# A long-convolution and MLP kernel: k's transposing loads moved to SP's queue, products of zeros at the start, V's write as one transfer, and a new written-out order

## The chip, the cores and the metric

The kernel runs on one core of a Trainium2 chip. The metric is the time of one execution in device microseconds (us); of several executions the median is taken. A profiled execution gives, besides its time, its span from the first to the last instruction, and a trace.

## The reference

Two layers are applied twice, with the same weights and the same k and v (S = 2048 tokens, D = 512, F = 1376, everything bf16):

```python
def _A_ref(q, k, v, shift_k, ssm_k, ssm_D):
    for t in range(ks):                       # ks = 4
        k_shift = k_shift + k_pad[:, t:t + S, :] * shift_k[:, ks - 1 - t][None, None, :]
    kv = k_shift * v
    # y = causal convolution of kv with the filter ssm_k along S, by rfft of length 2S
    y = y + kv * ssm_D[None, None, :]
    return q * y
def _B_ref(x, w1, b1, w2, b2):
    y = _layernorm(x, axis=-1)
    h = _gelu(jnp.einsum("bsd,df->bsf", y, w1) + b1)
    return jnp.einsum("bsf,fd->bsd", h, w2) + b2

x = A_q
x = x + _A_ref(_layernorm(x), ...)
x = x + _B_ref(_layernorm(x), ...)
x = x + _A_ref(_layernorm(x), ...)
x = x + _B_ref(_layernorm(x), ...)
```

The convolution does not depend on x, so its result is computed once and used in both layers.

## The kernel before, in words

Tokens are handled in two halves of 1024 (h = 0, 1). The convolution is a transform in two matrix stages with fixed tables (F, W, M, M2, G), a product with the filter's transform, and the way back; the MLP is two matrix products with gelu between.

Work is cut into some 600 pieces. `plan.add` (L142) notes a piece with its engine and code, and a table of words at the top of the file, ORDER, says in which order the pieces are written (L148). A word is name.engine: P is TensorE, D VectorE, A ScalarE, G GpSimd, S the queue of SyncE (SP), from which the DMA transfers go; digits behind it choose a buffer. Each engine, and each queue, carries out its pieces in the order of the table and waits at a piece until what it needs is there. Names end in e where a piece empties PSUM (L269 to L273).

The pieces that matter here, first at the start:

- **lK00, lK01** load the first half of the filter ssm_k, **lF**, **lG**, **lW**, **lM2**, **lM** the tables, **lv0** the first half of v (1 MB), all through L327. **lk00, lk01** load the first half of k with a transposing DMA (L395 to L398); they are issued from ScalarE's queue. Behind them on ScalarE stands **tab** (L400), a first gelu, which loads the activation table. **lK10, lK11** (L437) bring the filter's second half with transposing transfers, and **KR10, KR11** ("the turns", L442) move it on within SBUF.
- **KT00, KT01** (L427) transpose the filter on TensorE. **K00S0 to K03S1** (L356) are the first stage of its transform, **K0T0 to K0T3** (L370) transposes behind it; VectorE and ScalarE empty PSUM after each (L273 and L271). **dt0, dt1** add ssm_D. **col, cole** turn the short filter shift_k into columns, **dg0 to dg3** (GpSimd, L470) make diagonal matrices of them, and **kv00 to kv03** (L487) make k_shift with these on TensorE; VectorE multiplies with v (L493).
- **KW** (L502) is the second stage for the filter, **wa** ("the swaps", L512) exchange partitions within SBUF, **U** and **X** are the two stages for kv, **T** the products with the filter's transform (L561).

Then, for the second half of the tokens, the way back:

- **V10 to V17** (L583) go from the product to 512 columns; ScalarE empties each (V10e to V17e) into one half of a buffer of 512 KB. **vw10 to vw13** (L592 to L595) write these buffers, two V's each, to a DRAM tensor vd: vw10 that of V10 and V11, up to vw13 that of V16 and V17. **vr10 to vr13** (L603) read vd in another arrangement and need all four writes; **Y10 to Y13** (L614) multiply what they brought.
- The rows go through layers i = 0 to 7, each a group of 512 tokens in one layer. **sa, pa, na, aa, ga, sb, pb, nb, ab** with i and 0 or 2 are the norms and the product with Y. **dw** (L685) writes the normed rows to DRAM tensors lnd, **dr** (L688) reads them back with a transposing DMA, **m1** (L700) and **m2** (L717) are the two matrix products, **ge** (L707) the gelu, **re** (L721) the sum, **st** (L730) the store. A trailing digit counts parts.

For V's write the layout matters: the buffer has 128 partitions, of which the first 64 (par = 0) and the last 64 (par = 1) belong to two interleaved halves of vd:

```python
vdr = [dram.tile([64, 2, NK, D], BF16, name=f"vd{i}") for i in range(2)]
```

So 64 partitions write 64 rows of vd that lie 2 * NK * D elements apart.

Of the kernel before, what the change touches and what calls it, by code (L numbers as in the profile page):

```python
# [9 lines left out]
BF16 = mybir.dt.bfloat16  # L10
# [6 lines left out]
lK01.S lK00.S lF.S lk01.A lG.S lv0.S lK10.S lk00.A KT01.P0 lW.S tab.A lK11.S KT00.P1 KT01e.D dt1.D lM2.S K02S0.P0  # L17
KT00e.D col.P2 K02S0e.A0 K03S0.P3 cole.D K03S1.P1 K03S0e.A1 dt0.D dg0.G K03S1e.D K00S0.P2 K00S1.P0 K00S0e.A2 K01S0.P3
K00S1e.D K01S1.P1 K01S0e.A3 K0T3.P2 dg3.G K01S1e.D K02S1.P0 K0T3e.A K0T0.P3 K02S1e.D KR10.S K0T1.P1 K0T0e.D dg1.G
K0T2.P2 K0T1e.A kv00.P3 K0T2e.D kv03.P0 dg2.G kvm00.D KW01.P2 KW03.P1 KW01e.A kvm03.D kv01.P3 KW03e.A KW02.P2 kvm01.D  # L20
kv02.P0 KW02e.A KW00.P1 kvm02.D U01S0.P3 KW00e.A KR11.S KW04.P2 KW04e.D U01S0e.A0 U00S0.P0 U00S1.P1 U00S0e.A3 U01S1.P3
U00S1e.D wa00.S U02S0.P2 U01S1e.A U03S0.P0 U02S0e.D2 U02S1.P1 U03S0e.A1 U03S1.P3 U02S1e.D KW07.P2 U03S1e.A KW05.P0
ones0.G kS.G KW07e.D KW05e.A KW06.P1 U0T0.P3 KW06e.A U0T2.P2 U0T0e.D4 wa01.S U0T1.P1 U0T2e.D5 X00.P3 X01.P0 U0T1e.D6
X00e.A U0T3.P2 X01e.A lx0.S T00.D0 X04.P3 X02.P1 X02e.A X03.P0 lk11.S T01.D1 X03e.A V00.P1 U0T3e.D6 X04e.A V01.P0 w3.S
T02.D0 V00e.A X06.P3 X07.P2 X06e.A w4.S T03.D1 V02.P1 lk10.S V01e.A T06.D2 X05.P3 X07e.A V03.P0 T04.D0 lM.S X05e.A
V06.P2 T07.D1 V02e.A V04.P3 V03e.A T05.D2 V07.P1 V04e.A sa12.D V05.P0 V07e.A K1S6.P3 lv1.S sa02.D V05e.A w2.S K1S2.P1
# [10 lines left out]
re03.D pb20.G sa22.D m110.P3 ge12.A Tb16.D2 pa22.G m114.P1 ge10.A U1r2.S1 Ta16.D1 lx1.S X10e.A0 X11.P3 nb20.D aa22.D
V16.P0 U1r1.S5 X11e.A1 Tb10.D0 m113.P2 ge14.A ga22.D V16e.A6 m111.P1 Ta10.D1 ge13.A Ta11.D2 V10.P0 ge11.A X17.P2
Tb11.D0 m115.P3 X17e.A0 X14.P1 Ta17.D1 ge15.A V11.P2 V10e.A0 Tb17.D0 m210.P3 X14e.A1 sb22.D V11e.A ab20.A V17.P2
Tb14.D2 pb22.G X15.P1 m212.P0 X15e.A0 dw20.S re10.D vw10.S nb22.D Ta14.D0 V17e.A ab22.A Ta15.D1 V14.P2 X12.P1 Tb15.D0  # L40
dw22.S V14e.A1 vw13.S X12e.A1 Ta12.D2 V15.P2 X13.P1 Tb12.D0 V15e.A dr2.S X13e.A0 Ta13.D1 V12.P2 vw12.S Tb13.D0 V12e.A5
sa30.D V13.P2 m213.P1 V13e.A sa42.D vw11.S re12.D pa42.G m211.P2 pa30.G na42.D sa40.D aa42.A m121.P0 re11.D vr13.S5
sa50.D vr12.S1 m122.P2 ge21.A vr10.S6 vr11.S0 sa32.D pa50.G m123.P0 ge22.A re13.D pa40.G sa52.D Y13.P2 pa32.G Y13e.A
aa40.D Y12.P1 m124.P2 ga42.D Y12e.A pa52.G ge23.A ga40.D m120.P1 ge24.A sb42.D m125.P0 ge20.A sb40.D pb42.G Y11.P2
Y10.P3 ge25.A Y10e.A m223.P0 aa32.D pb40.G na30.D ab42.D aa30.A dw42.S ones1.G ab40.D Y11e.A m221.P3 ga30.D dw40.S
sb30.D m222.P2 dr4.S re23.D pb30.G na50.D ga32.D m220.P0 nb30.D sb32.D ab30.A aa52.D aa50.A pb32.G dw30.S m144.P1
# [16 lines left out]
NK = 16  # L63
# [100 lines left out]
def kernel(ctx: ExitStack, tc: tile.TileContext, A_q, A_k, A_v, A_shift_k, A_ssm_k, A_ssm_D,  # L164
# [75 lines left out]
    IDt = const.tile([P, P], BF16, name="IDt")  # L240
    sR = const.tile([CT, KS * P], BF16, name="sR")
# [9 lines left out]

    nc.gpsimd.memset(IDt[:], 1.0)
# [68 lines left out]
    plan = _Plan()  # L321
    add = plan.add
    with tc.tile_pool(name="ps", bufs=1, space=bass.MemoryType.PSUM) as ps:
        pf = [ps.tile([P, 1024], F32, name=f"p{i}") for i in range(NPS)]

        def load(name, dst, src, nbytes, deps=(), **info):
            return add(name, "S", deps, lambda it: queue(it["eng"]).dma_start(dst, src), nbytes=nbytes, **info)  # L327
# [214 lines left out]
        for h in range(2):  # L542
            vws, v0 = [], None
            for j in range(NT):
# [47 lines left out]
                def leave(it, z=v0, h=h, j=j):  # L592
                    for par, rows in enumerate(HALVES):
                        queue(it["eng"]).dma_start(vdr[h][:, par, 2 * j - 2:2 * j + 2, :], zt(z)[rows, :, :])
# [170 lines left out]
```

## Time and profile before

| what | us |
|---|---|
| median of three runs | 252.04 |
| lowest and highest of them | 251.12, 255.55 |
| the profiled execution | 249.63 |
| its span | 247.9 |
| TensorE busy in the span | 229.6 |
| VectorE busy | 167.2 |
| ScalarE busy | 152.7 |

A row of the timeline gives the start, the duration, the engine, the line, the operation, what it writes and reads, how many instructions are merged, and in brackets the idle time ahead of it with what ended it. ACT is ScalarE, DVE VectorE, PE TensorE, PEld its weight loads, POOL GpSimd, SPq and ACTq the DMA issues of SyncE and ScalarE. p stands for PSUM, arena for the large SBUF tensor that holds nearly everything.

### The profile page before, as it was taken

The page shows a single profiled execution, that of the slowest core. Times are in us where ns is not written, and L with a number is a line of the kernel's source. Part 1 is how long each engine was busy: PE and PEld are TensorE (multiplying, and loading weights), DVE is VectorE, ACT ScalarE, POOL GpSimd, SP SyncE. Part 2 cuts the span into 40 slices and gives each one's busy share as a digit, 9 for nine tenths or more (in the row PEclk, how much of TensorE's full clock was granted, in tenths as well). Part 3 has the DMA queues.
Part 4 walks back from the last instruction along what each step waited for, and adds up shares of the span by engine and source line. Part 5 has one row for each costly group of instructions (what it writes and reads, how often), then busy time and mean ns, then how long its engine had stood idle before and what let it go on. Part 6 is the DMA issues. An engine that isn't in the chain of part 4 may idle for free.

```text
span 247.9 us, 4244 instructions
## 1 busy us (share of the span) xinstructions
PE 229.6 (93%) x1654; PEld 120.8 (49%) x1654; DVE 167.2 (67%) x305; ACT 152.7 (62%) x197; POOL 45.4 (18%) x91
## 2 busy tenths in 40 slices
PE   1879998999999999997798999999999999999993
PEld 1759766885554444343343444444444444444441
DVE  0748999999996689899988999401697764001232
ACT  0186969999999477999557933875027824572200
POOL 1392000041404015011043421300121211000000
PEclk9979999999999999999999999999999999999999
DMA  6979999999679999967948153615000066500033
GB/s 201 317 178 276 151 206 229 177 319 376 281 283 318 320 280 221 246 159 218 223 117 292 48 123 102 112 51 118 0 3 1 0 175 184 109 0 0 3 78 92
DMA packets 46358, 40.81 MB, mean 165 GB/s; under 512 B 28828, under 2 KB 41602, under 8 KB 45186
## 3 DMA queue, kind: packets, MB, share of 16 engines
q1 hardware_dynamic: 41826, 39.22, 59.8%
q10 hardware_dynamic: 4512, 1.32, 2.5%
q8 instruction: 13, 0.21, 0.4%
q14 instruction: 7, 0.06, 0.1%
HBM read 16.41 MB, written 12.06 MB: 115 GB/s over the span
## 4 chain that ended last, share of the span: by engine, by line
PE 76%; DVE 11%; ACTq 4%; ACT 3%; DMA 2%; issue 1%; POOL 1%; SPq 0%; DVEq 0%
PE p L717 29%; PE p L700 29%; ACTq L396 4%; PE p L370 3%; DVE arena L561 3%; PE p L487 3%; PE p L457 3%; PE p L502 2%; ACT arena L271 2%; DVE arena L493 2%; PE p L583 2%; PE p L570 2%; DMA arena<-vd 2%; DVE arena L273 2%; DVE lst L291 1%
## 5 line engine op out<-in xcount | busy, mean ns | idle before, releaser
L271 ACT ACTIVATE arena<-p 128x1024 bf16<-128x1024 f32 (+1 forms) x79 | 79.1, 1092 | 15.1 <-PE p L502 7.5
L707 ACT ACTIVATE arena<-p,B 128x512 bf16<-128x512 f32 (+1 forms) x88 | 53.8, 690 | 39.9 <-PE p L700 39.8
L717 PE MATMUL p<-arena 128*128 128x512 bf16 (+1 forms) x352 | 78.2, 379 | 0.1
L700 PE MATMUL p<-arena 128*128 128x512 bf16 (+1 forms) x352 | 77.8, 379 | 0.0
L721 DVE TENSOR_TENSOR arena<-p,arena 128x512 bf16<-128x512 f32 x32 | 21.4, 682 | 53.9 <-PE p L717 53.9
L700 PEld LDWEIGHTS <-arena 128*128 128x128 bf16 (+1 forms) x352 | 34.8, 100 | 41.7 <-issue 1.6
L717 PEld LDWEIGHTS <-arena 128*128 128x128 bf16 (+1 forms) x352 | 34.0, 98 | 43.0 <-issue 2.5
L291 DVE BATCH_NORM_STATS2 lst<-arena 128x6 f32<-128x512 bf16 x64 | 40.8, 680 | 0.3
L298 POOL TENSOR_SCALAR lrs<-lmv 128x2 f32<-128x2 f32 x32 | 9.3, 290 | 136.1 <-DVE lmv L293 135.3
L309 ACT ACTIVATE arena<-arena,lnm,lrs 128x512 bf16<-128x512 bf16 x28 | 21.3, 823 | 11.6 <-DVE lnm L303 11.6
L561 DVE TENSOR_TENSOR arena<-arena 128x2048 bf16<-128x2048 bf16 x24 | 28.1, 1218 | 0.3 <-PE p L583 0.2
L300 POOL TENSOR_TENSOR lrs<-lrs,mhalf 128x2 f32<-128x2 f32 x32 | 24.8, 776 | 2.7
L273 DVE CAST arena<-p 128x1024 bf16<-128x1024 f32 x13 | 15.5, 1221 | 5.8 <-PE p L356 4.1
L273 DVE COPY arena<-p 128x2048 bf16<-128x2048 bf16 (+1 forms) x12 | 13.3, 1131 | 8.1 <-PE p L427 6.4
L311 DVE TENSOR_SCALAR arena<-arena,lmv,lrs 128x512 bf16<-128x512 bf16 x36 | 13.3, 411 | 2.3 <-POOL lrs L300 2.2
L666 DVE TENSOR_TENSOR arena<-arena 128x1024 bf16<-128x1024 bf16 x16 | 10.9, 682 | 2.4 <-ACT arena L309 1.2
L356 PE MATMUL p<-Ft,arena 128*128 128x256 bf16 x64 | 10.1, 308 | 2.5 <-ACT arena L271 2.4
L457 PE MATMUL p<-arena,Ft 128*128 128x512 bf16 x48 | 11.6, 379 | 0.3 <-DVE arena L493 0.3
L502 PE MATMUL p<-arena,Wt 64*64 64x512 bf16 x128 | 11.0, 389 | 0.6 <-DVE arena L273 0.5
L667 DVE TENSOR_TENSOR arena<-arena 128x1024 bf16<-128x1024 bf16 x16 | 11.1, 692 | 0.6
L583 PE MATMUL p<-arena 64*64 64x512 bf16 x128 | 8.4, 380 | 2.9 <-ACT arena L271 2.0
L470 POOL TENSOR_SCALAR arena<-IDt,sF 128x128 bf16<-128x128 bf16 x16 | 9.3, 599 | 9.1 <-DVE B L273 9.1
(43 smaller groups left out, 118.8 us busy)
## 6 DMA issues: line engine op xcount, KB each, us to landing
arena<-arena SPq DMA_DIRECT2D x16, 256.0 KB, 5.6
zd<-arena SPq DMA_DIRECT2D x8, 512.0 KB, 3.6
arena<-zd SPq DMA_DIRECT2D x8, 512.0 KB, 6.1
lnd<-arena SPq DMA_DIRECT2D x14, 256.0 KB, 2.2
arena<-in_A_v_dram SPq DMA_DIRECT2D x2, 1024.0 KB, 6.0
arena<-in_A_q_dram SPq DMA_DIRECT2D x4, 512.0 KB, 7.4
vd<-arena SPq DMA_DIRECT2D x8, 256.0 KB, 3.5
arena<-vd SPq DMA_DIRECT2D x4, 512.0 KB, 4.2
```

Source lines behind the costliest of these rows:

```text
L271: nc.scalar.activation(dst, src, AF.Copy)
L273: nc.vector.tensor_copy(dst, src)
L291: nc.vector.bn_stats(lst[:, i, :], xg[:, i, :])
L300: nc.gpsimd.tensor_tensor(self.rs[:, a:b], self.rs[:, a:b], mhalf[:, a:b], ALU.pow)
L309: nc.scalar.activation(dst[:, i, :], xg[:, i, :], AF.Identity, bias=self.nm[:, i:i + 1], scale=rs)
L457: nc.tensor.matmul(o[:, gh, :], Ft[:, t + gh, :], src[:, n, :], start=x == 0, stop=x == len(parts) - 1)
L502: nc.tensor.matmul(o[cols, par, :], Wt[rows, 2 * j + kk, :], z[rows, kk, :], start=True, stop=True)
L561: nc.vector.tensor_tensor(Tb[it["slot"]["T"]].rearrange("p s a d -> p s (a d)"), x2, kk, ALU.mult)
L700: nc.tensor.matmul(o[0:m, x, :], W1t[:, ct, ft * P:ft * P + m], lt[:, ct, :], start=ct == 0, stop=ct == CT - 1)
L707: nc.scalar.activation(ht[0:m, ft, :], o[0:m, x, :], AF.Gelu_apprx_tanh, bias=B1[0:m, ft:ft + 1])
L717: nc.tensor.matmul(o, ht[0:m, ft, t * P:t * P + P], W2t[0:m, ft, :], start=ft == 0, stop=ft == FT - 1)
L721: nc.vector.tensor_tensor(xg[:, t, :], view(pf[pe["slot"]["ps"]], [D]), xg[:, t, :], ALU.add)
```

## The change

The table ORDER is new; its first line shows the kind of difference, the rest is left out:

```diff
-lK01.S lK00.S lF.S lk01.A lG.S lv0.S lK10.S lk00.A KT01.P0 lW.S tab.A lK11.S KT00.P1 KT01e.D dt1.D lM2.S K02S0.P0
+lK01.S lK00.S lF.S lv0.S lk00.S KT01.P0 lk01.S KT01e.D KT00.P1 dt1.D col.P0 KT00e.D K02S0.P2 K03S0.P3 K02S0e.A0 cole.D
...
     IDt = const.tile([P, P], BF16, name="IDt")
+    idle = const.tile([P, P], BF16, name="idle")
...
+    nc.vector.memset(idle[:], 0.0)
     nc.gpsimd.memset(IDt[:], 1.0)
...
     nc.vector.memset(first[:, 0:1], 0.0)
+    nc.scalar.activation(first[:, 1:2], first[:, 0:1], AF.Gelu_apprx_tanh)
...
         pf = [ps.tile([P, 1024], F32, name=f"p{i}") for i in range(NPS)]
+
+        for i in range(38):
+            nc.tensor.matmul(pf[NPS - 1][:, 0:P], idle[:], idle[:], start=True, stop=True)
...
-        lk = [[add(f"lk{h}{q}", "S" if h else "A", [], lambda it, h=h, q=q: queue(it["eng"]).dma_start_transpose(
+        lk = [[add(f"lk{h}{q}", "S", [], lambda it, h=h, q=q: queue(it["eng"]).dma_start_transpose(
...
-        tab = add("tab", "A", [], lambda it: nc.scalar.activation(first[:, 1:2], first[:, 0:1], AF.Gelu_apprx_tanh), after=lk[0], ns=1350)
...
-                pe = add(f"kv{h}{cc}", "P", lk[h] + [dg[cc]], mms, take=["ps"], pe_ns=870, mode=1)
+                pe = add(f"kv{h}{cc}", "P", lk[h] + [dg[cc]], mms, take=["ps"], pe_ns=1000, mode=1)
...
                 def leave(it, z=v0, h=h, j=j):
-                    for par, rows in enumerate(HALVES):
-                        queue(it["eng"]).dma_start(vdr[h][:, par, 2 * j - 2:2 * j + 2, :], zt(z)[rows, :, :])
-                vws.append(add(f"vw{h}{j // 2}", "S", [v0, ev], leave, free=[(v0, "zt")], nbytes=2 ** 19, write=True, nd=2, half=1))
+                    queue(it["eng"]).dma_start(apf(vdr[h], vdr[h].offset + (2 * j - 2) * D, [[NK * D, 2], [2 * NK * D, 64], [1, 4 * D]]), zt(z))
+                vws.append(add(f"vw{h}{j // 2}", "S", [v0, ev], leave, free=[(v0, "zt")], nbytes=2 ** 19, write=True))
```

In words: lk00 and lk01 go out from SP's queue, behind lv0; the gelu that loads the table stands ahead of all pieces on ScalarE; TensorE multiplies a 128x128 tile of zeros with itself 38 times, into a PSUM buffer that is overwritten later; each vw is one transfer instead of two. The number pe_ns only informs whoever made the table. The file's lines from the zeros on lie a few further down.

ScalarE's first instructions, before. L396 is k's transposing load, p a PSUM buffer that L271 empties:

```order
L254 DMA arena<-in_A_ssm_D_dram 1x512
L255 DMA sR<-in_A_shift_k_dram 4x512
L256 DMA b1R<-in_B_b_dram 10x128
L257 DMA b1L<-in_B_b_dram 1x96
L396 DMA_TRANSPOSE arena<-in_A_k_dram 128x4x512
L396 DMA_TRANSPOSE arena<-in_A_k_dram 128x4x512 [waits DMAHW1_49]
L400 ACT_TABLE_LOAD
L400 ACTIVATE first<-first 128x1 [waits DVE_49]
L271 ACTIVATE arena<-p_150 128x4x2x128 [waits DVE_49,PE_49]
```

And now:

```order
L256 DMA arena<-in_A_ssm_D_dram 1x512
L257 DMA sR<-in_A_shift_k_dram 4x512
L258 DMA b1R<-in_B_b_dram 10x128
L259 DMA b1L<-in_B_b_dram 1x96
L263 ACT_TABLE_LOAD
L263 ACTIVATE first<-first 128x1 [waits DVE_49]
L275 ACTIVATE arena<-p_155 128x4x2x128 [waits PE_49]
```

The two transposing loads have left ScalarE, and its first emptying (K02S0e) stands right behind the table.

SP's first instructions, before (tabF, tabW and tabM are tables, L437 is lK10 and lK11):

```order
L327 DMA arena<-in_A_ssm_k_dram 128x2x1024 x2
L327 DMA Ft<-tabF 128x768
L327 DMA Gt<-tabG 128x64 [waits DMAHW0_49]
L327 DMA arena<-in_A_v_dram 128x4096 [waits DMAHW2_49]
L437 DMA_TRANSPOSE arena<-in_A_ssm_k_dram 128x4x512 [waits DMAHW6_49,DMAHW3_49,DMAHW1_49]
L327 DMA Wt<-tabW 128x1024 [waits DMAHW4_49]
L437 DMA_TRANSPOSE arena<-in_A_ssm_k_dram 128x4x512 [waits DMAHW5_49]
L327 DMA arena<-tabM 128x4096
```

And now:

```order
L334 DMA arena<-in_A_ssm_k_dram 128x2x1024 x2
L334 DMA Ft<-tabF 128x768
L334 DMA arena<-in_A_v_dram 128x4096
L403 DMA_TRANSPOSE arena<-in_A_k_dram 128x4x512 [waits DMAHW0_49]
L403 DMA_TRANSPOSE arena<-in_A_k_dram 128x4x512 [waits DMAHW1_49]
L442 DMA_TRANSPOSE arena<-in_A_ssm_k_dram 128x4x512 [waits DMAHW2_49]
L334 DMA Wt<-tabW 128x1024 [waits DMAHW3_49]
L442 DMA_TRANSPOSE arena<-in_A_ssm_k_dram 128x4x512 [waits DMAHW4_49]
L334 DMA arena<-tabM 128x4096 [waits DMAHW5_49]
```

k's loads stand behind v's and ahead of the filter's second half; the load of G has gone further down.

SP around V's write, before, from the second half of vw10 on (L594 is vw, L685 dw22, L688 dr2, L603 vr; the shape is that of the DRAM side, slowest extent first):

```order
L594 DMA vd_146<-arena 64x2048 [waits DMAHW0_49]
L685 DMA lnd_135<-arena 128x2x512 [waits DMAHW1_49,DVE_49,Activation_49]
L594 DMA vd_146<-arena 64x2048 [waits DMAHW2_49]
L594 DMA vd_146<-arena 64x2048 [waits DMAHW3_49]
L688 DMA_TRANSPOSE arena<-lnd_135 128x4x512 [waits DMAHW6_49,DMAHW4_49,DMAHW1_49]
L594 DMA vd_146<-arena 64x2048 [waits DMAHW5_49,Activation_49]
L594 DMA vd_146<-arena 64x2048
L594 DMA vd_146<-arena 64x2048 [waits DMAHW7_49,Activation_49]
L594 DMA vd_146<-arena 64x2048 [waits DMAHW0_49]
L603 DMA arena<-vd_146 128x4x512 [waits DMAHW5_49,DMAHW3_49,DMAHW6_49,DMAHW2_49,DMAHW7_49,DMAHW0_49,PE_49]
```

And now (L598 is vw, L689 dw20 and dw22, L692 dr2, L607 vr):

```order
L598 DMA vd_149<-arena 2x64x2048 [waits DMAHW6_49,Activation_49]
L598 DMA vd_149<-arena 2x64x2048 [waits DMAHW7_49]
L689 DMA lnd_138<-arena 128x2x512 [waits DMAHW0_49,DVE_49,Activation_49]
L689 DMA lnd_138<-arena 128x2x512 [waits DMAHW1_49,DVE_49,Activation_49]
L598 DMA vd_149<-arena 2x64x2048 [waits DMAHW2_49,Activation_49]
L692 DMA_TRANSPOSE arena<-lnd_138 128x4x512 [waits DMAHW3_49,DMAHW1_49,DMAHW0_49]
L598 DMA vd_149<-arena 2x64x2048 [waits DMAHW4_49,Activation_49]
L607 DMA arena<-vd_149 128x4x512 [waits DMAHW5_49,DMAHW6_49,DMAHW4_49,DMAHW7_49,DMAHW2_49,PE_49]
```

vw13 now goes first, ahead of vw10, dw20 and dw22; then vw12, dr2, vw11 and the reads, as before. The transposing dr2 waits for dw20 and dw22, the first read for all four writes. On TensorE the products behind V13 are m211, m213, m123, m122, Y13, m121, Y12, m120, m124, m125, Y11, Y10, m222; before they were m213, m211, m121, m122, m123, Y13, Y12, m124, m120, m125, Y11, Y10, m223. On ScalarE V17e came behind ab20, and X12e behind both; now X12e comes first, then V17e, then ab20.

More of the change, by code (lines that the diff above doesn't have):

```diff
@@ L16 @@
 ORDER = """
-lK01.S lK00.S lF.S lk01.A lG.S lv0.S lK10.S lk00.A KT01.P0 lW.S tab.A lK11.S KT00.P1 KT01e.D dt1.D lM2.S K02S0.P0
[L18 to L26, printed above, removed]
@@ L37 @@
[L37 to L46, printed above, removed]
@@ new lines @@
+Ta12.D1 ab22.A V15.P1 X13.P3 Tb12.D0 V15e.A dw22.S X13e.A2 Ta13.D2 vw12.S V12.P1 Tb13.D0 V12e.A3 dr2.S sa40.D V13.P1
+m211.P3 V13e.A sa30.D pa40.G vw11.S re12.D m213.P1 sa42.D sa32.D pa42.G vr13.S3 m123.P2 vr12.S2 re10.D vr10.S1 re11.D
+vr11.S6 m122.P0 ge23.A re13.D na42.D sa50.D aa42.A Y13.P2 m121.P1 sa52.D pa50.G Y13e.A ge22.A aa40.D pa30.G Y12.P2
+ga42.D m120.P3 Y12e.A pa52.G ge21.A ga40.D m124.P2 pa32.G ge20.A sb42.D m125.P1 ge24.A sb40.D pb42.G Y11.P3 Y10.P0
+ge25.A Y10e.A m222.P1 pb40.G ab42.D Y11e.A na50.D na30.D dw42.S aa32.D ones1.G ab40.D aa30.A m220.P3 ga32.D dw40.S
@@ L58 @@
+st61.S m263.P2 ge71.A ge74.A m262.P1 re63.D m271.P2 re62.D st63.S st51.S m273.P1 m270.P3 re73.D re71.D st73.S m272.P2
+re70.D st70.S st71.S re72.D st72.S
 """
```

54 lines of the change are left out of this document (33 added, 21 removed).

## Prediction

> **What bounds the kernel now.** I read the page first, then stretches of the span, the chain of waits, and the timelines around the two places that the change touches. The page's share of busy time and its chain, by engine, say that TensorE sets the time:
>
> ```profile
> span 247.9 us, 4244 instructions
> PE 229.6 (93%) x1654; PEld 120.8 (49%) x1654; DVE 167.2 (67%) x305; ACT 152.7 (62%) x197; POOL 45.4 (18%) x91
> ...
> PE 76%; DVE 11%; ACTq 4%; ACT 3%; DMA 2%; issue 1%; POOL 1%; SPq 0%; DVEq 0%
> ```
>
> The average hides stages. The busy time by stretch (columns: length, then PE, PEld, DVE, ACT, POOL busy) shows them:
>
> ```profile
> 21.30:39.50 18.20, 16.84 (x238) 12.71 (x237) 16.95 (x15) 14.27 (x16) 0.20 (x1) 1.00 1.05 206
> ...
> 121.30:139.20 17.90, 16.77 (x86) 7.13 (x83) 16.05 (x42) 11.26 (x16) 6.32 (x15) 1.00 0.59 180
> 139.20:244.00 104.80, 104.73 (x484) 47.58 (x483) 50.16 (x116) 46.62 (x73) 13.31 (x27) 1.00 0.28 67
> ```
>
> From 139.2 us on TensorE stands still for 0.07 us in 104.8: whatever delays it before that point delays the end by as much. Earlier it is the engines that empty PSUM that are full, VectorE for 16.95 of 18.20 us from 21.3 on. The chain at the start runs elsewhere:
>
> ```profile
> 2.33 4.14 ACTq L396
> ...
> 6.51 5.02 ACTq L396
> ...
> 13.06 0.92 ACT arena L271
> ```
>
> ScalarE issues k's two transposing transfers (L396), loads its table (L400), and only at 13.06 empties the first PSUM tile that TensorE waits for.
>
> **The front: transposes to SP, table early, zeros.** ScalarE no longer issues L396. Its first emptying, K02S0e, then follows K02S0 on TensorE:
>
> ```profile
> 5.18 3.63 PE L427 MATMUL p<-IDt,arena 128*128 128x128 bf16 x32 [5.18 <-DMA arena<-in_A_ssm_k_dram]
> 8.74 1.03 PE L356 MATMUL p<-Ft,arena 128*128 128x256 bf16 x4
> 14.02 2.78 PE L356 MATMUL p<-Ft,arena 128*128 128x256 bf16 x12 [2.40 <-ACT arena L271]
> 15.14 1.23 DVE L273 CAST arena<-p 128x1024 bf16<-128x1024 f32 x1 [2.69 <-PE p L356]
> 32.91 3.21 PE L370 MATMUL p<-IDt,arena 128*128 128x128 bf16 x48
> ```
>
> K02S0 ends at 9.77, so ScalarE starts 13.06 - 9.77 = 3.3 us earlier; the VectorE row also loses its 2.7 us wait. The filter's stage is bound by these two engines emptying PSUM together: 6.0 us of freed time over two engines is 3.0 us. I take -3.0, with ends of 0 (another transfer is late next) and -6.0 (the two add up). The table load itself costs nothing: it now runs while ScalarE would wait for K02S0 anyway.
>
> The 38 products of zeros: the 32 transposes above take 3.63 / 32 = 113 ns each, those at 32.91 only 3.21 / 48 = 67 ns, so TensorE starts slow. 38 x 113 ns = 4.3 us, started near 1 us after VectorE's memset, ends near 5.3: about where the filter lands (5.18). Cost 0 to 0.2 us. Their gain, at most 32 x 46 ns = 1.5 us of TensorE, lies under the emptying; I take 0.
>
> SP now issues lk00 and lk01 where it used to wait. Behind them stand lK11, lW, lK10, lM2 and the filter's second half. The two issues (4.14 + 5.02 us by the chain) begin near 2.8 and end near 12; before, SP got to lK10 only at 13.45:
>
> ```profile
> 13.45 1.88 SPq L437 DMA_TRANSPOSE arena<-in_A_ssm_k_dram  x1
> ```
>
> So what is queued there is about a microsecond early, not late. k itself comes behind v's 1 MB; that is a rival below.
>
> **V's write.** Before, each of four pieces (512 KB) went as two transfers of 64 partitions; now as one of 128, whose DRAM side is led by an extent of 2 (2x64x2048 in the order). ScalarE's emptyings set when the pieces can go, SP issues them, and TensorE waits for them at Y13:
>
> ```profile
> 109.80 1.52 ACT L309 ACTIVATE arena<-arena,lnm,lrs 128x512 bf16<-128x512 bf16 x2
> 111.41 1.94 ACT L271 ACTIVATE arena<-p 128x1024 bf16<-128x1024 f32 x2
> ...
> 116.96 2.37 SPq L688 DMA_TRANSPOSE arena<-lnd  x1
> 119.44 4.12 SPq L594 DMA_DIRECT2D vd<-arena  x4
> 127.44 2.69 SPq L603 DMA_DIRECT2D arena<-vd  x4
> ...
> 121.30 4.93 PE L717 MATMUL p<-arena 128*128 128x512 bf16 x22
> 126.07 5.34 PE L700 MATMUL p<-arena 128*128 128x512 bf16 x24
> 131.65 0.62 PE L614 MATMUL p<-arena,Gt 128*64 128x512 bf16 x4 [0.24 <-DMA arena<-vd]
> 133.13 0.62 PE L614 MATMUL p<-arena,Gt 128*64 128x512 bf16 x4 [0.86 <-DMA arena<-vd]
> ```
>
> Y13 (131.65) came only 0.24 us after TensorE was ready: there is almost no slack. What one transfer with such a shape costs no row shows, since before has none; the bulk transfers that it has are led by 16 or more on both sides. The page's list of DMA issues (KB each, median us to landing) gives the nearest:
>
> ```profile
> arena<-arena SPq DMA_DIRECT2D x16, 256.0 KB, 5.6
> zd<-arena SPq DMA_DIRECT2D x8, 512.0 KB, 3.6
> ...
> vd<-arena SPq DMA_DIRECT2D x8, 256.0 KB, 3.5
> arena<-vd SPq DMA_DIRECT2D x4, 512.0 KB, 4.2
> ...
> arena<-arena SPq DMA_DIRECT2D x8, 128.0 KB, 7.6
> ```
>
> The one end: spread over all 16 DMA engines like zd, the same bytes from the same 128 partitions, 3.6 us; of the issues that are saved one lies on the path, that of the last piece's second half: vw12 and vw11 took 4.12 us for four with a wait among them, so it is 1.0 at most and 0 at least, and I take -0.5. The other end: the transfer is divided by its leading extent, and 2 of 16 engines carry it. At the same or half the size the landing grows as the lead shrinks: vd (led by 64) 256 KB in 3.5, the swaps (32) 256 KB in 5.6, the turns (16) 128 KB in 7.6 us. These come from different stages, so it is a hint and no proof, but by leading extent the turns are the nearest row to 2, and they are the slowest. I take the two-engine end. [...]
>
> What one engine moves is bounded by two stretches (last columns: DMA share and GB/s):
>
> ```profile
> 9.00:10.00 1.00, 1.00 (x10) 0.52 (x8) 1.00 (x1) 0.00 (x0) 0.00 (x0) 1.00 0.94 393
> 119.40:123.00 3.60, 2.69 (x24) 1.37 (x25) 3.60 (x8) 1.88 (x2) 0.00 (x0) 1.00 1.05 248
> ```
>
> 393 / 16 = 24.6 GB/s, and 248 / 16 = 15.5 with vd's own writes under way. Half of 512 KB is 262144 bytes: 10.7 or 16.9 us for a piece. With fourteen engines idle I take 10.7. The four pieces queue on the same two engines: 42.7 us. Also through these go their sixteenths of dw20, dw22 (0.7 us each) and dr2 (1.3): 2.7.
>
> The path, step by step: V17e ends at 111.41 + 1.94 = 113.35. In the new order ScalarE's pass ab20 (the 1.52 us at 109.80) stands behind it and X12e (half of 1.94) ahead: -0.5; with the front's -3.0, vw13 goes at 109.85. Start and receipt: zd's 3.6 less 524288 B / 393 GB/s = 1.3 is 2.3. So the last piece has landed at 109.85 + 2.3 + 42.7 + 2.7 = 157.55, and vr13, at 4.2, feeds Y13 at 161.75 instead of 131.65: +30.1.
>
> Queued behind: SP holds dr2 until dw22 has landed, past vw13 and vw10, near 109.85 + 2.3 + 21.4 + 1.4 = 135; vw11 and all of vr behind it. That costs no more, since vw12 still runs on the two engines then. But m123 and m122 wait for dr2, past vw12 as well, until about 147, so they no longer fill TensorE after V13. After Y13 the new order has m121 still to do (+1.7), which covers the 0.86 wait at 133.13: +0.8. After such idleness TensorE runs slow again, as it did after the 2.4 us pause that ended at 14.02 (third column from the right: the granted clock):
>
> ```profile
> 14.02:21.30 7.28, 7.28 (x80) 6.30 (x80) 4.81 (x4) 5.56 (x5) 6.32 (x12) 0.79 1.02 230
> ```
>
> 7.28 x 0.21 = 1.5 us lost.
>
> **The sum**, against the profiled execution's own 249.6 us (span 247.9 and 1.7 around it; the median of the runs, 252.0, lies 2.4 above): 249.6 + 30.1 + 0.8 + 1.5 = 282.0. The rest of the new order I price at nothing: behind Y13 it holds the same products, and TensorE is full there.
>
> **The rivals.** (a) All sixteen engines carry V's write. Then only the front and the saved issue count: 249.6 - 3.0 - 0.5 = 246.1, 1.4% below. For it speaks zd's row, against it the row of landings by lead. (b) The same, and the front's freed time adds up instead of being shared: 249.6 - 6.0 - 0.5 = 243.1, 2.6% below. It decides if the first kv product (L487) starts 6 us earlier than before; against it, VectorE and ScalarE are busy for 16.95 and 14.27 of the 18.20 us that follow. (c) Sixteen engines, and k lands late: its transposes stand behind v's 1 MB on one queue, and what the front gains, the first kv product loses, at most the 3.0: 249.1. For it, the queue is in order; against it, SP ends their issue near 12, as ScalarE did.
>
> **How the numbers follow.** Two engines: 0.82. Sixteen, (a): 0.11; (b): 0.05; (c): 0.02. The time is that of the first, 282. Its lower end takes the front at -6.0 (-3.0), no extra start and receipt (-2.3), no slow clock (-1.5) and 393 / 0.94 / 16 = 26.1 GB/s (-2.6): 272.6, rounded down to 271 for what the new order may save where TensorE is not full. Its upper end takes 16.9 us for a piece, 4 x 6.2 = 25: 307, or 308. From 271 to 308 leaves out only the three rivals, 0.18. Two per cent is 5 us, about what a measurement of this kernel tells from no change: slower is the first case, 0.82; the same (a) and (c), 0.13; faster (b), 0.05.
>
> **What would show it.** Right: the list of DMA issues has vd<-arena x4 at 512 KB with a landing over 10 us, growing along the four; L614 waits for the DMA of vd for more than 10 us; the DMA share falls to about 2/16 between. Wrong: a landing of 4 to 5 us there. The front is right if ScalarE's first L271 starts before 10 us and the first L487 at least 2 us earlier than before, and wrong if L487 waits for k's transposes. The zeros are right if the first L427 products take about 67 ns and start within 0.3 us of the filter's landing.

## The result, and the profile after

The changed kernel takes 292.24 us (median of four runs, 289.23 to 294.36), the kernel before 251.58 (250.02 to 255.55) beside it: a ratio of 1.160, with a 95% interval of 1.145 to 1.175. Slower was forecast, and 292.24 lies inside the forecast range, 10.2 us above the 282 that was forecast. The profiled execution took 291.16 us. (Of the experiments below, e5, whose median is 253.57 us, was profiled in an execution of 259.47 us at a granted clock of 0.938, so the times read from that profile are rough.) The page of the changed kernel, the same lines as before:

```profile
span 289.4 us, 4299 instructions
...
PE 235.3 (81%) x1671; PEld 124.3 (43%) x1692; DVE 168.7 (58%) x307; ACT 153.4 (53%) x196; POOL 44.9 (16%) x91
...
PE 44%; DMA 24%; SPq 17%; DVE 6%; ACT 5%; issue 3%; DVEq 0%; ACTq 0%
```

TensorE's work is the same but for the products of zeros; the span around it is 41.5 us longer, and the chain that ended last, 76% TensorE before, now runs through the DMA and SP's issues for 41%. Busy time by stretch (length, then PE, PEld, DVE, ACT, POOL busy; the last three columns are the granted clock, the DMA share, that is the mean busy share of the sixteen DMA engines, and GB/s) shows where:

```profile
126.70:154.06 27.36, 4.73 (x24) 2.03 (x23) 10.64 (x30) 1.02 (x1) 5.43 (x12) 0.64 0.57 85
135.00:141.00 6.00, 0.00 (x0) 0.00 (x0) 2.34 (x9) 0.00 (x0) 3.67 (x8) 0.50 0.13 52
154.06:178.80 24.74, 15.24 (x60) 5.71 (x62) 5.77 (x13) 10.08 (x16) 0.99 (x3) 0.78 0.32 105
178.80:285.50 106.70, 104.49 (x474) 47.59 (x483) 50.70 (x116) 47.05 (x73) 12.70 (x27) 1.00 0.27 67
```

The second row is the heart of it. From 135 to 141 us no product runs, hardly anything but V's write is under way, and the DMA share is 0.13: two of sixteen engines would be 0.125. 52 GB/s are moved, 26 GB/s for each of two. Of the 100 packets in that stretch 32 hold less than 2 KB and so are not V's, whose rows have 4 KB. What TensorE waits for, in its timeline, and SP's queue behind it:

```profile
126.89 4.70 PE L721 MATMUL p<-arena 128*128 128x512 bf16 x21 [0.16 <-issue]
154.06 5.62 PE L704 MATMUL p<-arena 128*128 128x512 bf16 x16 [22.47 <-DMA arena<-lnd]
168.94 1.06 PE L618 MATMUL p<-arena,Gt 128*64 128x512 bf16 x4 [9.26 <-DMA arena<-vd]
```

```profile
117.79 1.22 SPq L598 DMA_DIRECT2D vd<-arena  x2
119.61 10.64 SPq L689 DMA_DIRECT2D lnd<-arena  x2
130.35 2.43 SPq L598 DMA_DIRECT2D vd<-arena  x1
142.13 9.80 SPq L692 DMA_TRANSPOSE arena<-lnd  x1
152.03 0.52 SPq L598 DMA_DIRECT2D vd<-arena  x1
165.03 2.67 SPq L607 DMA_DIRECT2D arena<-vd  x4
```

(L598 is vw, L689 dw20 and dw22, L692 dr2, L607 vr, L618 Y, L704 m1, L721 m2.) The first idle stretch, 22.47 us, is not booked to V's write at all: m123 waits for dr2, and dr2, issued at 142.13, for dw22, which went out behind the first two vw: the small packets among V's from 135 to 141 us are taken for the last of lnd's. Only the second, 9.26 us, names vd. Both have one cause, as e1 below shows. The start of the kernel, ScalarE and then TensorE:

```profile
8.70 3.77 ACT L275 ACTIVATE arena<-p 128x1024 bf16<-128x1024 f32 x4 [4.87 <-PE p L363]
```

```profile
1.05 3.94 PE L331 MATMUL p<-idle 128*128 128x128 bf16 x38 [1.05 <-DVE first L262]
5.14 1.21 PE L432 MATMUL p<-IDt,arena 128*128 128x128 bf16 x16
6.62 1.21 PE L432 MATMUL p<-IDt,arena 128*128 128x128 bf16 x16 [0.27 <-DMA arena<-in_A_ssm_k_dram]
...
16.12 2.06 PE L492 MATMUL p<-arena 64*128 64x256 bf16 x42
```

The first emptying comes 4.3 us earlier than before (12.96), the first kv product 5.2 us earlier (21.30), and there is no wait for k. Yet none of it arrives: the first m1 product starts at 70.42 (70.66 before), and the first vw goes out at 117.79 (111.81 before).

### The profile page after: what moved, and what is told of

It reads as the page before. It is cut to its first block, busy times and chain, and to the rows that moved or that the text cites. A ratio compares the mean times of both kernels' runs of the same rounds, so it can differ in the third digit from the quotient of the medians.

```text
span 289.4 us, 4299 instructions
## 1 busy us (share of the span) xinstructions
PE 235.3 (81%) x1671; PEld 124.3 (43%) x1692; DVE 168.7 (58%) x307; ACT 153.4 (53%) x196; POOL 44.9 (16%) x91
## 4 chain that ended last, share of the span: by engine, by line
PE 44%; DMA 24%; SPq 17%; DVE 6%; ACT 5%; issue 3%; DVEq 0%; ACTq 0%
PE p L704 21%; PE p L721 17%; SPq L403 6%; DMA lnd<-arena 6%; DMA vd<-arena 4%; SPq L692 3%; DMA arena<-lnd 3%; PE p L588 3%; SPq L517 2%; ACT arena L711 2%; DMA arena<-zd 2%; DMA arena<-in_A_ssm_k_dram 2%; SPq L447 2%; DMA zd<-arena 2%; ACT arena L275 2%
## 5 line engine op out<-in xcount | busy, mean ns | idle before, releaser
L704 PE MATMUL p<-arena 128*128 128x512 bf16 (+1 forms) x344 | 81.8, 393 | 24.6 <-DMA arena<-lnd 23.9
L721 PE MATMUL p<-arena 128*128 128x512 bf16 (+1 forms) x343 | 77.6, 379 | 0.8 <-issue 0.2
L704 PEld LDWEIGHTS <-arena 128*128 128x128 bf16 (+1 forms) x352 | 35.6, 103 | 69.8 <-DMA arena<-lnd 24.3
L721 PEld LDWEIGHTS <-arena 128*128 128x128 bf16 (+1 forms) x352 | 34.0, 98 | 42.8 <-issue 2.7
L302 POOL TENSOR_SCALAR lrs<-lmv 128x2 f32<-128x2 f32 x32 | 8.6, 269 | 171.6 <-DVE lmv L297 153.8
L566 DVE TENSOR_TENSOR arena<-arena 128x2048 bf16<-128x2048 bf16 x24 | 28.4, 1220 | 7.7 <-DMA arena<-arena 4.1
L304 POOL TENSOR_TENSOR lrs<-lrs,mhalf 128x2 f32<-128x2 f32 x32 | 24.0, 751 | 2.7
L277 DVE CAST arena<-p 128x1024 bf16<-128x1024 f32 x15 | 18.0, 1219 | 1.1 <-PE p L363 0.5
L277 DVE COPY arena<-p 128x2048 bf16<-128x2048 bf16 (+1 forms) x11 | 12.3, 1125 | 8.1 <-PE p L432 5.4
L618 PE MATMUL p<-arena,Gt 128*64 128x512 bf16 x32 | 4.9, 417 | 9.3 <-DMA arena<-vd 9.3
L498 DVE TENSOR_TENSOR arena<-p,arena 128x1024 bf16<-128x1024 f32 x8 | 9.5, 1214 | 2.7 <-PE p L618 2.3
```

The source lines that it names most:

```text
L277: nc.vector.tensor_copy(dst, src)
L304: nc.gpsimd.tensor_tensor(self.rs[:, a:b], self.rs[:, a:b], mhalf[:, a:b], ALU.pow)
L566: nc.vector.tensor_tensor(Tb[it["slot"]["T"]].rearrange("p s a d -> p s (a d)"), x2, kk, ALU.mult)
L704: nc.tensor.matmul(o[0:m, x, :], W1t[:, ct, ft * P:ft * P + m], lt[:, ct, :], start=ct == 0, stop=ct == CT - 1)
L721: nc.tensor.matmul(o, ht[0:m, ft, t * P:t * P + P], W2t[0:m, ft, :], start=ft == 0, stop=ft == FT - 1)
```

## The experiments

Two questions are apart: what V's write costs and why, and where the front's gain went. The letters of the theories hold within each group. Each kernel was run beside the kernel before on the same chip, and each ratio is to that.

### V's write: as many engines as the DRAM side's leading extent?

Theory A: one transfer led by 2 runs on two engines; led by 128 it would run on all. The rival: one large transfer is slow as such, or the time lies in the new order.

**e1_two_transfers**: the changed kernel, V's write as before.

```diff
-                    queue(it["eng"]).dma_start(apf(vdr[h], vdr[h].offset + (2 * j - 2) * D, [[NK * D, 2], [2 * NK * D, 64], [1, 4 * D]]), zt(z))
+                    for par, rows in enumerate(HALVES):
+                        queue(it["eng"]).dma_start(vdr[h][:, par, 2 * j - 2:2 * j + 2, :], zt(z)[rows, :, :])
```

> The changed kernel with one part undone: V's pieces are written as two transfers of 64 partitions each, led by 64, as before the change. Theory A (a transfer is carried by as many DMA engines as its leading extent allows, so the one led by 2 ran on two engines): the writes land within about 4 us of their issue, vr is issued about 5 us after V13 has been emptied (before: 122.4 to 127.4) instead of 37, Y13 stands near 137 instead of 168.9, and the time is 291 - 32 - 2 (slow clock) = 256 to 258. Theory B (the new order, not the shape of the transfer, holds up TensorE before Y13): the wait of L704 for the DMA of lnd (22.5 us) stays for the most part, and the time stays above 275.

Measured: 257.39 us against 251.94, a ratio of 1.025 (1.016 to 1.034). Its m1 and Y13 on TensorE:

```profile
132.69 3.62 PE L705 MATMUL p<-arena 128*128 128x512 bf16 x16
137.38 0.62 PE L619 MATMUL p<-arena,Gt 128*64 128x512 bf16 x4 [1.07 <-DMA arena<-vd]
```

Of the two waits of 22.47 and 9.26 us, 1.07 us is left. V's write as one transfer is thus 292.24 - 257.39 = 34.9 us of the loss; the other 5.5 are the rest of the change.

**e2_before_one_transfer**: the reverse, the kernel before with this one edit.

> The kernel before, with V's pieces written as one transfer led by 2 and nothing else changed. Theory A: four pieces at 11.4 us on two engines (512 packets took from 119.0 to 164.6 in the changed kernel) from 113.0 on, with 2.7 for the others' shares: the last lands near 161, Y13 stands near 165 instead of 131.7, and with 1.5 for the slow clock the time is 250 + 34 + 1.5 = 285 (280 to 290). Theory B: the old order has room for it; within 5 us of before.

Measured: 284.50 us, a ratio of 1.136 (1.122 to 1.150). SP (L593 vw, L687 dr2, L602 vr) and TensorE:

```profile
111.89 0.63 SPq L593 DMA_DIRECT2D vd<-arena  x1
...
125.53 9.79 SPq L687 DMA_TRANSPOSE arena<-lnd  x1
...
158.54 2.67 SPq L602 DMA_DIRECT2D arena<-vd  x4
```

```profile
137.47 7.94 PE L699 MATMUL p<-arena 128*128 128x512 bf16 x24 [11.16 <-DMA arena<-lnd]
162.63 1.06 PE L613 MATMUL p<-arena,Gt 128*64 128x512 bf16 x4 [17.23 <-DMA arena<-vd]
```

In the old order nearly the same 46.65 us pass from the first vw to the first vr (47.24 in the changed kernel). How TensorE's waiting divides between dr2 and vr depends on the order: 11.16 and 17.23 us here, 22.47 and 9.26 there, in sum 28.4 and 31.7.

**e3_one_transfer_led_by_128**: still one transfer of 128 partitions per piece, but vd laid out so that row p belongs to partition p; the reads go in halves to suit.

```diff
-                    queue(it["eng"]).dma_start(apf(vdr[h], vdr[h].offset + (2 * j - 2) * D, [[NK * D, 2], [2 * NK * D, 64], [1, 4 * D]]), zt(z))
+                    queue(it["eng"]).dma_start(apf(vdr[h], vdr[h].offset + (2 * j - 2) * D, [[NK * D, 128], [1, 4 * D]]), zt(z))
...
-                    queue(it["eng"]).dma_start(zt(it), apf(vdr[h], vdr[h].offset + 16 * q * 2 * NK * D, [[D, 2 * NK], [2 * NK * D, 16], [1, D]]))
+                    for par, rows in enumerate(HALVES):
+                        queue(it["eng"]).dma_start(zt(it)[rows, :, :], apf(vdr[h], vdr[h].offset + (par * 64 + 16 * q) * NK * D, [[D, NK], [NK * D, 16], [1, D]]))
```

> The changed kernel with V's pieces still written as one transfer of 128 partitions, but into a DRAM tensor laid out so that its side is led by 128; the reads vr are split in two halves of 64 partitions instead. Theory A: the landing is that of zd's writes (3.3 us), and the time is that of the kernel with two transfers within 2 us. Theory C (one transfer of 512 KB with 4 KB rows is slow whatever leads it, for instance by its bytes for each engine): the landing stays over 10 us and the time above 280.

Measured: 257.17 us, a ratio of 1.025 (1.013 to 1.037), the time of the two transfers. SP, from the first vw to the first vr:

```profile
117.15 0.82 SPq L598 DMA_DIRECT2D vd<-arena  x2
...
130.42 5.17 SPq L608 DMA_DIRECT2D arena<-vd  x8
```

13.3 us in place of 47.2, with as many writes and bytes; a write lands in 3.6 us (list of DMA issues), near theory A's 3.3. That one transfer takes the place of two is neither the harm nor a gain; the shape is the harm.

**e4_one_transfer_led_by_4** and **e12_one_transfer_led_by_8**: as e3, with the DRAM side led by 4 and by 8, and the reads in halves to suit (shown is the write of the first; the second has 8, 8 and 16).

```diff
+                    queue(it["eng"]).dma_start(apf(vdr[h], vdr[h].offset + (2 * j - 2) * D, [[NK * D, 4], [4 * NK * D, 32], [1, 4 * D]]), zt(z))
```

> As the one led by 128, but the DRAM tensor is laid out so that the transfer is led by 4. Theory A: four engines carry it, the DMA share while only these writes move is 4/16 = 0.25 at about 95 GB/s, a piece takes 5.7 us, and the time lies between: 291 - 22 = 269, give or take 4. A theory that knows only a fast and a slow form (a leading extent of 16 or more, or less) gives the time of the changed kernel, about 290, or that of the one led by 128.

> As the run e4_one_transfer_led_by_4, with the DRAM side of each write led by 8 (8x16x2048), so that by theory A eight of the sixteen engines carry it: between the first and the last write a DMA share near 0.5 and about 190 GB/s where nothing else moves, 2.8 us for a piece of 512 KB. The last of the four can only go when V13 is emptied, so the time falls almost to that of the changed kernel with two transfers: 258, from 257 to 260. Rival H (a leading extent below 16 stalls SP's in-order queue whatever its size, as dr2 and vw11 stood behind vw10 with 4): 262 or more, with the issue of dr2 over 5 us and TensorE waiting for the DMA of lnd or vd for over 5 us.

Measured: 279.56 us with 4 (one run) and 267.79 with 8, a ratio of 1.061 (1.051 to 1.071). Both shares are as theory A said. The stretch of 4, in which some of lnd's packets still go out, then that of 8, while SP issues dw20 and dw22 (121.24 to 125.69):

```profile
132.00:138.00 6.00, 1.86 (x9) 0.66 (x7) 6.00 (x17) 0.00 (x0) 1.10 (x4) 0.98 0.26 95
```

```profile
122.00:124.00 2.00, 2.00 (x24) 0.79 (x23) 1.44 (x3) 1.48 (x3) 0.42 (x1) 1.00 0.48 98
```

So 2, 4 and 8 give shares of 0.13, 0.26 and 0.48. The rates are 52, 95 and 98 GB/s (with 8, 141 from 130 to 132 us at the same share of 0.48): the 190 that was expected with 8 did not come, and why is open. Both times were missed, by some 10 us each: the forecasts counted the write's duration and not the queue behind it. SP with 4, then TensorE with 8:

```profile
136.74 6.26 SPq L693 DMA_TRANSPOSE arena<-lnd  x1
143.10 0.55 SPq L598 DMA_DIRECT2D vd<-arena  x1
153.35 5.17 SPq L608 DMA_DIRECT2D arena<-vd  x8
```

```profile
137.48 6.45 PE L705 MATMUL p<-arena 128*128 128x512 bf16 x16 [4.26 <-DMA arena<-lnd]
146.44 0.90 PE L619 MATMUL p<-arena,Gt 128*64 128x512 bf16 x4 [2.51 <-DMA arena<-vd]
```

With 4, vw11 stands on SP behind dr2 and goes only at 143.10, so that the last piece starts that late; the DMA share is 0.30 from 144 to 150 us, and 0.26 from 150 to 156, where the reads begin (153.35). With 8, TensorE loses 4.26 and 2.51 us in waits, and the 16 products that follow the first take 6.45 us instead of e1's 3.62. Rival H, which said 262 or more, was nearer in time, though its dr2 issue of over 5 us was 2.86 and its waits of over 5 us were these two.

### The front: where 5 us go

**e5_front_alone**: the kernel before with the front (lk00 and lk01 on SP behind lv0, the table early, the zeros), old order and two transfers otherwise. The edits beside the table are those of the change.

```diff
-lK01.S lK00.S lF.S lk01.A lG.S lv0.S lK10.S lk00.A KT01.P0 lW.S tab.A lK11.S
+lK01.S lK00.S lF.S lG.S lv0.S lk01.S lk00.S lK10.S KT01.P0 lW.S lK11.S
```

> The kernel before with the front alone: lk00 and lk01 go from SP's queue behind lv0, the gelu that loads the table stands first on ScalarE, the 38 products of zeros stand at the start; the rest of the table stays, and V is written in two transfers of 64 partitions. Theory A (the front's gain is real, and it was the new order between 36 and 70 us that gave it back): ScalarE's first emptying before 10 us, the first kv product 3 to 5 us earlier than 21.30, and the end 2 to 4 us earlier than before, about 248.5. Rival B (the DMA engines, busy for a share of about 1.0 from 10 to 60 us in every profile, give the time of that stretch, whatever the order; the front's gain is lost there anyway): the first kv product early, but the first V0 product at 39.5 as before and the time 252 within 1.

Measured: 1.003 (0.998 to 1.007) times the kernel before: nothing gained, as rival B said; the first V0 product started at 40.40 (39.51 before). SP's turns (L447) and swaps (L517), and VectorE's first product T00:

```profile
19.21 7.52 SPq L447 DMA_DIRECT2D arena<-arena  x8
27.16 7.50 SPq L517 DMA_DIRECT2D arena<-arena  x8
```

```profile
39.12 2.36 DVE L566 TENSOR_TENSOR arena<-arena 128x2048 bf16<-128x2048 bf16 x2 [5.96 <-DMA arena<-arena]
```

VectorE is ready 4.5 us earlier than before (33.16 for 37.64) and waits for the swaps. Before, it did not. The changed kernel has the same wait, shorter, since its order puts one turn behind a swap:

```profile
34.64 1.22 DVE L566 TENSOR_TENSOR arena<-arena 128x2048 bf16<-128x2048 bf16 x1 [1.50 <-DMA arena<-arena]
```

**e9_front_turns_behind_swaps**: e5 with the turns KR10 and KR11 issued behind both swaps; and **e10_front_turns_behind_swaps_and_q** with them behind lx0 too.

```diff
-K01S1.P1 K01S0e.A3 K0T3.P2 dg3.G K01S1e.D K02S1.P0 K0T3e.A K0T0.P3 K02S1e.D KR10.S K0T1.P1
+K01S1.P1 K01S0e.A3 K0T3.P2 dg3.G K01S1e.D K02S1.P0 K0T3e.A K0T0.P3 K02S1e.D K0T1.P1
...
-kv02.P0 KW02e.A KW00.P1 kvm02.D U01S0.P3 KW00e.A KR11.S KW04.P2
+kv02.P0 KW02e.A KW00.P1 kvm02.D U01S0.P3 KW00e.A KW04.P2
...
-U0T0e.D4 wa01.S U0T1.P1
+U0T0e.D4 wa01.S KR10.S KR11.S ones0.G kS.G U0T1.P1
```

> The kernel of the run e5_front_alone with one thing moved: the turns KR10 and KR11 (the filter's second half, needed only at 50 us) go out on SP behind both swaps wa00 and wa01 instead of ahead of them. There VectorE stood at its first product T00 for 5.96 us, waiting for the swaps, whose issues began at 27.16 and ended at 34.66. Theory F (the turns ahead of the swaps gave the front's gain back): the swaps go out from about 23.5, the wait at T00 falls below 2 us, the first V0 product starts before 37, and the time is 248 to 250. Rival G (the DMA engines, at a share of about 1.0 up to 60 us, only pass the wait on: the turns, q or the second half of k land later): the first V0 product before 37 all the same, but a new wait between 45 and 60 us for a DMA, the first m1 product at 70 to 71, and 252 within 1.

> As the last, with the turns also behind lx0, the first half of q, which the first norms need at 47.8 us. Theory F: 248 to 250, as the last. Rival G: the first stage of the filter's second half (K1S6) waits for the turns, and the time is 252 to 254.

Measured: 253.68 us, a ratio of 1.010 (1.004 to 1.016), and 259.82, a ratio of 1.033 (1.027 to 1.040). e9 went rival G's way. VectorE (L566 is T00, L294 the first norm) and TensorE (L575 the first V0, L492 the kv of the second half):

```profile
33.13 2.35 DVE L566 TENSOR_TENSOR arena<-arena 128x2048 bf16<-128x2048 bf16 x2
...
49.97 1.29 DVE L294 BATCH_NORM_STATS2 lst<-arena 128x6 f32<-128x512 bf16 x2 [6.54 <-DMA arena<-in_A_q_dram]
```

```profile
34.99 1.97 PE L575 MATMUL p<-arena 128*128 128x128 bf16 x32 [0.59 <-ACT arena L274]
...
55.28 3.44 PE L492 MATMUL p<-arena 64*128 64x256 bf16 x44 [4.42 <-DMA arena<-in_A_k_dram]
```

The wait for the swaps is gone, and the first V0 product starts at 34.99 instead of 39.51. Then q is 6.54 us late, and k 4.42; the second half's kv starts at 55.28 (54.56 before), and the first m1 product at 74.03 (70.66 before); rival G said 70 to 71 there, and a time of at most 253. e10 missed. Its wait for the turns came as rival G said, 4.55 us ahead of K1S6, but its time lies 5.8 us above G's 254:

```profile
51.87 4.26 PE L462 MATMUL p<-arena,Ft 128*128 128x512 bf16 x12 [4.55 <-DMA arena<-arena]
```

Its first V0 product came at 37.78 and not at 34.99, with a wait of 1.86 us for lW at 20.22, where its table is still that of e9: executions differ by some 2 us in this part. In e9 and e10 the wait is passed on from one transfer to the next. In the kernel before the DMA share was high already:

```profile
20.00:30.00 10.00, 9.87 (x153) 7.81 (x151) 8.83 (x8) 7.78 (x8) 0.39 (x1) 1.00 1.08 202
30.00:40.00 10.00, 8.76 (x117) 6.62 (x116) 9.41 (x10) 7.88 (x9) 0.20 (x1) 1.00 0.96 209
40.00:50.00 10.00, 9.28 (x141) 7.57 (x138) 10.00 (x13) 10.00 (x12) 0.00 (x0) 1.00 1.05 190
50.00:60.00 10.00, 9.69 (x130) 7.50 (x129) 9.21 (x18) 9.42 (x11) 3.56 (x8) 1.00 1.08 349
```

A share of about 1.0 for forty microseconds, at some 200 GB/s in the first thirty, half of the 393 from 9 to 10 us; 3053 of the 4681 packets from 20 to 50 us hold less than 512 bytes. Work that was ready sooner there only waited sooner. But a share of 1.0 does not prove that the engines can do no more (the last section has one of 1.06 at 67 GB/s), so that they are the limit is argued, not shown. A rival is SP's queue, which issues in order: in e9 the first half of q goes out behind the turns, at 39.56 instead of 37.47. Issuing part of these transfers from another queue was not tried.

**e11_e9_without_zeros**: e9 without the 38 products of zeros.

```diff
-        for i in range(38):
-            nc.tensor.matmul(pf[NPS - 1][:, 0:P], idle[:], idle[:], start=True, stop=True)
```

> The kernel of e9_front_turns_behind_swaps without the 38 products of zeros. If the zeros only warm TensorE for work that the emptying of PSUM hides: the transposes of the filter at 113 ns again, the first kv product within 0.4 us of that with the zeros, and the time the same within 0.5%. If they count: up to 1.5 us later at the first kv product, and as much at the end.

Measured: 253.97 us against e9's 253.68, both 1.010 times the kernel before. Without them, then with them:

```profile
4.91 3.63 PE L430 MATMUL p<-IDt,arena 128*128 128x128 bf16 x32 [4.91 <-DMA arena<-in_A_ssm_k_dram]
...
17.66 2.14 PE L490 MATMUL p<-arena 64*128 64x256 bf16 x44
```

```profile
5.08 2.97 PE L432 MATMUL p<-IDt,arena 128*128 128x128 bf16 x32
...
16.77 2.15 PE L492 MATMUL p<-arena 64*128 64x256 bf16 x44
```

They bring the first kv product forward by 0.89 us, more than the 0.4 expected of a hidden effect, and the end by nothing that can be seen.

### The new order

Three tables were joined from the two: **e6_after_to_first_V0_then_before** and **e7_after_to_first_m1_then_before** (the changed kernel with two transfers; new order up to the piece named, then the old for what is left) and **e8_before_to_first_m1_then_after** (the kernel before; old order first, then the new). The joint of e8, where the words of the old order end and those of the new begin:

```diff
-U1S6e.D5 m102.P2 U1S7e.A ga12.D m104.P1 aa10.A U1w3.S K1r1.S sb12.D K1r2.S U1S4e.A0 m100.P0 K1r0.S ga10.D pb12.G
+U1S6e.D5 m102.P2 U1S7e.A ga12.D m104.P1 U1S2.P0 U1S2e.D1 U1w3.S aa10.A U1S3.P0 U1S3e.D K1r1.S m101.P0 ge04.A K1r0.S
```

> The changed kernel with V's write in two transfers; its table is the new one up to the first V0 products (V01, V00; 119 pieces), and from there on all pieces that are left stand in the old order. In the profiles the first V0 product started at 35.9 with the new order and at 39.5 with the old. Theory A (the new order's first part gains 3.6 us, the stretches behind lose it): 248, from 247 to 250. Rival B (the gain is lost behind it whatever the order, since the DMA engines are full to 60 us): 252 within 1.

> As the last, but the new table holds up to the first m1 products (m104; 224 pieces), and the old order from there on. The first m1 started at 70.42 with the new order, at 70.66 with the old. Theory A (what the front gained is lost by then, and what is lost beyond is lost behind it): 251.5, from 250.5 to 253. Rival D (the new order's first part leaves transfers and buffers late, so that the loss behind m1 comes from what stands ahead of it): 255 to 258, the changed kernel's time with two transfers.

> The reverse: the kernel before (its front, its transfers of V), with the old table up to its first m1 products and the new one for the pieces that are left. Theory A (the new order loses 5 to 6 us between the first m1 and Y13 by itself): 257 to 258. Rival D (it loses them because of what its own first part left late): 252 to 253.

Measured: 256.33, 255.55 and 258.92 us, ratios of 1.014 (1.004 to 1.024), 1.014 (1.007 to 1.021) and 1.026 (1.019 to 1.034). e6 missed both its theories, and e7 lies at the lower end of rival D's 255 to 258: the new first part, with the old order behind it, costs 1.4%. e8 lies 0.9 us above theory A's 258: the new order behind the first m1 costs as much as the whole change does with two transfers (1.025). But a joined table has a joint that neither order has, and what the joint costs was not measured apart. TensorE in e8, m1 (L700) among the first stage for kv (L457), up to the first V1:

```profile
76.70 0.59 PE L457 MATMUL p<-arena,Ft 128*128 128x512 bf16 x2 [1.37 <-DVE arena L273]
78.61 6.21 PE L700 MATMUL p<-arena 128*128 128x512 bf16 x28 [1.31 <-DVE arena L273]
...
106.93 1.06 PE L583 MATMUL p<-arena 64*64 64x512 bf16 x16
```

Before, the 44 m1 products ran without a pause from 70.66 on, and the first V1 started at 99.68. In e8 TensorE waits for emptyings between them, the norms' write dw10 goes out at 83.46 instead of 78.00, the swaps of the second half at 94.19 instead of 90.30, and V1 is 7.25 us later; 76 m1 products stand ahead of it, 68 before. The pauses at 76.70 and 78.61 come just behind the joint, and e1, with the new order throughout, has neither. There V1 starts at 107.44, and the longest wait ahead of it is one that the kernel before does not have, for zd, the DRAM tensor through which the first stage's result is regrouped:

```profile
98.20 0.64 PE L507 MATMUL p<-arena,Wt 64*64 64x512 bf16 x4 [2.69 <-DMA arena<-zd]
```

So the new order costs some 5 us, but which of its moves costs them is open. The two losses, 1.4% and 2.6%, don't add up in the changed kernel; why was not tried.

## Why the prediction was right, and what it mis-sized

By the steps of its sum:

| step | predicted | measured |
|---|---|---|
| first vw issued | 109.85 | 117.79 |
| first vw to first vr | 47.7 | 47.24 |
| first vr to Y13 | 4.2 | 3.91 |
| Y13 to the end of the span | 118.55 | 120.46 |
| span | 280.3 | 289.4 |

The predicted 118.55 is 247.9 - 131.65 = 116.25 before, plus the terms of 0.8 and 1.5; the differences, +7.94, -0.46, -0.29 and +1.91, are the 9.1 us between the spans.

**V's write: right in mechanism and size.** For the division by the leading extent the forecast had three landings from different stages, by its own words a hint and no proof. The runs agree with it: shares of 0.13, 0.26 and 0.48 with leads of 2, 4 and 8, and no loss with 128. One transfer of 128 partitions in place of two halves cost 34.9 us led by 2, and led by 128 (e3) it neither cost nor saved (257.17 us against e1's 257.39). Of the forecast, 30.1 + 3.0 + 0.8 + 1.5 = 35.4 us are the write's (the 30.1 had the front's -3.0 in it), and it measured 34.9. Two sizes in it cancel, which is luck: by the 52 GB/s an engine of two moved 26 GB/s and not 24.6, so by estimate the four pieces take 40.3 us and not 42.7, while start, receipt and the other transfers took 47.24 - 40.3 = 6.9 and not 5.0. The wait at Y13, forecast at over 10 us, was 9.26; that the landings grow along the four the list of issues doesn't show, since it gives no landing for them. All three sixteen-engine rivals fall.

**The queue behind it: right.** dr2 waited for dw22, m123 for dr2. The forecast put dr2 near 135 and m123 near 147; shifted by the 7.94 they are 143 and 155, and were 142.13 and 154.06. It costs nothing beyond vr, as said: Y13 comes as long after the first vw as forecast.

**The front, -3.0: the step that failed,** together with "the rest of the new order I price at nothing". At its own place the front gained more than taken: 4.3 us at ScalarE's first emptying, 5.2 at the first kv product (the zeros gave 0.9 of it in e9; that the rest is the two engines' freed time nearly adding up was not tried). By the signs that the forecast named for it, the front was right. At the place where it counts, V's write, it gained nothing (e5). I had put "another transfer is late next" as one end of the term, 0, and taken -3.0 without asking which: the swaps, then q and k, in a stretch that the view showed at a DMA share of 1.05 from 21.3 to 39.5 us. That share stood in a row that I had quoted for VectorE. Rival (c), which had k land late, was not it: the first kv product had no wait for k.

**The new order at nothing: wrong.** With the front it is 5.5 us of the medians (e1). In the profiles Y13 is 137.38 - 131.65 = 5.7 us later in e1, and from there to the end it takes 256.6 - 137.38 = 119.2, 3.0 more than before (the profiled executions lie 8.7 apart, more than the medians). I argued only for what stands behind Y13, and even there TensorE now stands still for 106.70 - 104.49 = 2.2 us, where it lost 0.07; 1.4 us of that are two waits for lnd.

That 292.24 lies in the range is partly luck. Its upper end was set by pieces of 16.9 us, which did not come; for a front that gains nothing and an order that costs, which made most of the miss, it had no allowance.

**The slow clock, +1.5: right in size.** e2, with the old order, takes 280.6 - 162.63 = 118.0 us from Y13 to the end, 1.7 more than before; the first four Y products of it took 1.06 us, 0.62 before, and the mean granted clock of the execution is 0.943, 0.993 before. **The zeros at 0: right** for the time; 1.21 / 16 = 75 ns a product, not 67.

No kernel here beats the one before; e5, with a ratio of 1.003, is the nearest.

## What to carry to other kernels

Read a transfer's leading extent on the DRAM side before merging two transfers into one: two with a lead of 64 were 34.9 us faster here than one with a lead of 2, and the longest wait may be for another transfer (22.47 us for lnd in the changed kernel, 9.26 for vd). Where a stretch shows a DMA share near 1 (0.96 to 1.08 from 20 to 60 us in the kernel before, and e5's front came out at a ratio of 1.003), price a gain ahead of it at nothing until the next late transfer is named, and measure it at the place where the end is decided, not where the gain arises. A new order is not free because it holds the same work (with the front it was 5.5 us here): ask of each product that moved which emptying and which transfer it now stands ahead of.

## What the runs showed of the hardware that was not expected

- **SP's issues got long behind V's write.** dr2's transposing issue took 2.37 us on SP before, 2.30 in e1 and 3.02 in e3, but 9.80 and 6.26 us behind a lead of 2 and 4; with 8 it was 2.86. The engines that V's write leaves alone were not free meanwhile, as the stretch of the 9.80 us shows:

```profile
142.13:152.03 9.90, 0.00 (x0) 0.00 (x0) 0.00 (x0) 0.00 (x0) 0.00 (x0) 0.50 1.06 67
```

From 135 to 141 us, with little beside V's write, the share was 0.13 at 52 GB/s; here 641 of the 763 packets hold less than 512 bytes, which V's do not. By an estimate from the two rows dr2's own packets thus make up nearly all of the 1.06 and move only some 15 GB/s; that most of what the share counts there is waiting is argued from this, not shown.

- **The granted clock fell to 0.50 in a long pause.** It was 0.50 from 135 to 141 us. The 16 m1 products behind the pause of 22.47 us took 5.62 us, at a mean clock of 0.64, and those in e12 behind a pause of 4.26 us took 6.45, at 0.50 from 138 to 142 us and 0.69 from 142 to 144, for 3.62 at 1.00 in e1. The shorter pause cost no less, in one execution each.
